# Holding back a transposing load, and moving one weight load and the first sigmoid, at the start of a gated feed-forward kernel

## The chip, the core and the metric

The kernel runs on one NeuronCore of one Trainium2 chip. The metric is the device time of one execution in microseconds (us); lower is better. TensorE does the matrix products, VectorE (DVE) and ScalarE (ACT) the work on their results, GpSimd (POOL) a little set-up; SyncE (SP) and ScalarE issue the transfers (DMAs) between the chip's main memory and the on-chip memory, each from a queue of its own. All transfers run on the same 16 DMA engines.

## The reference

```python
# x (32, 32, 512), w1 and w3 (512, 1792), w2 (1792, 512), all bf16
gate = einsum("bsd,df->bsf", x, w1)
up   = einsum("bsd,df->bsf", x, w3)
out  = einsum("bsf,fd->bsd", silu(gate) * up, w2)
```

There are 1024 tokens of width 512, and a hidden width of 1792. silu(g) is g times sigmoid(g).

## The kernel before

All of the hidden state is kept turned: the 128 partitions carry 128 of the 512 or 1792 features, and the free dimension carries tokens. So x is needed as `xT` (four slabs `dt` of 128 input features by 1024 tokens). It arrives in two ways. The first 256 tokens are loaded as they lie (`x_sb`, two loads of 128 tokens, L68 and L69), turned on TensorE by products with the identity (`turned`, L106) and copied to `xT` by VectorE and ScalarE (`put`, L116, in the order of `plan`, L140: slab 0 of tokens 0 to 127 by VectorE, slab 0 of tokens 128 to 255 by ScalarE, slab 1 by VectorE, slabs 2 and 3 by ScalarE). The other tokens are turned by the transfer itself: tokens 256 to 511 by the transposing load at L74, tokens 512 to 1023 by that at L78. The text calls them the first and the second transposing load.

The weights are whole in on-chip memory. Of w1 and w3 the first four column blocks of 128 (`FK` = 4) come ahead of the others: w1 in four loads of one slab each (L71, 128 KB; slabs 0 and 2 on SP's queue, 1 and 3 on ScalarE's), w3 in two loads of two slabs each (L72 and L73, 256 KB, both on SP's queue). They are called the first w3 half and the second w3 half. Behind the first transposing load, SP issues the remaining columns of w1 and w3 (L76 and L77), the second transposing load and w2 (L80, L81).

The instructions of each engine keep the order in which they are written (`manual_schedule`, L47); the framework adds the semaphore waits. TensorE's order is: six products of constants (`keep_warm`, L139), the eight turning products, then for the first 256 tokens all sixteen gate products slab by slab over four column blocks (L145 to L147), the sixteen up products likewise (L149 to L151), then the same column blocks for tokens 256 to 511 (L152 to L154), then the blocks 4 to 13 of the first 512 tokens, all 14 blocks of the other 512 (L157 to L163), and the output products with w2 (L165 to L177). So the order of need on TensorE is: x, w1 slabs 0 to 3, w3 slabs 0 to 3, the first transposing load, the other columns of w1 and w3, and much later the rest.

ScalarE's order is: three transfers (one x half, w1 slabs 1 and 3), a sigmoid of one element a partition that only serves to load the table of the function (L85), its two copies of the turned x, and then the 28 sigmoids and seven of the output copies. A sigmoid, a product of gate and sigmoid (L135) and a product with up (L136) follow each column block.

Of the kernel before, what the change touches and what calls it, by code (L numbers as in the profile page):

```python
# [10 lines left out]
def kernel(  # L11
# [8 lines left out]
    nc = tc.nc  # L20
    P = nc.NUM_PARTITIONS
    fp32 = mybir.dt.float32
    bf16 = mybir.dt.bfloat16
    SIGMOID = mybir.ActivationFunctionType.Sigmoid
# [3 lines left out]
    N = B * S  # L28
    NB = 512
    HB = NB // 2  # L30
    DT = D // P
    FT = F // P
# [4 lines left out]
    x_flat = x.flatten_outer_dims()  # L37
    out_flat = out.flatten_outer_dims()
    w1_v = w1.rearrange("(dt p) f -> p dt f", p=P)
    w3_v = w3.rearrange("(dt p) f -> p dt f", p=P)  # L40
    w2_v = w2.rearrange("(ft p) d -> p ft d", p=P)

    consts = ctx.enter_context(tc.tile_pool(name="consts", bufs=1))
# [9 lines left out]
    xT = consts.tile([P, DT, N], bf16, name="xT")  # L53
    w1_sb = consts.tile([P, DT, F], bf16, name="w1_sb")
    w3_sb = consts.tile([P, DT, F], bf16, name="w3_sb")
    w2_sb = consts.tile([P, FT, D], bf16, name="w2_sb")
    hT = consts.tile([P, FT, N], bf16, name="hT")

    FK = 4

    def load_x(queue, t0, t1):
        queue.dma_start(out=x_sb[:, t0:t1, :], in_=x_view[:, t0:t1, :])  # L62

    def load_w(queue, w_sb, w_v, c0, c1, d0=0, d1=DT):
        f0, f1 = c0 * P, c1 * P
        queue.dma_start(out=w_sb[:, d0:d1, f0:f1], in_=w_v[:, d0:d1, f0:f1])  # L66

    load_x(nc.sync, 0, 1)  # L68
    load_x(nc.scalar, 1, 2)  # L69
    for dt in range(DT):  # L70
        load_w(nc.sync if dt % 2 == 0 else nc.scalar, w1_sb, w1_v, 0, FK, dt, dt + 1)  # L71
    load_w(nc.sync, w3_sb, w3_v, 0, FK, 0, 2)  # L72
    load_w(nc.sync, w3_sb, w3_v, 0, FK, 2, DT)  # L73
    nc.sync.dma_start_transpose(out=xT[:, :, HB:NB], in_=x_flat[HB:NB, :])  # L74
    for c0, c1 in ((FK, 8), (8, FT)):
        load_w(nc.sync, w1_sb, w1_v, c0, c1)  # L76
        load_w(nc.sync, w3_sb, w3_v, c0, c1)  # L77
    nc.sync.dma_start_transpose(out=xT[:, :, NB:N], in_=x_flat[NB:N, :])  # L78
    FH = FT // 2
    nc.sync.dma_start(out=w2_sb[:, 0:FH, :], in_=w2_v[:, 0:FH, :])  # L80
    nc.sync.dma_start(out=w2_sb[:, FH:FT, :], in_=w2_v[:, FH:FT, :])  # L81

    one = nc.const_aps.tensor(1.0, [P, 1], bf16)
    table = consts.tile([P, 1], fp32, name="table")
    nc.scalar.activation(table[:], one, SIGMOID)  # L85

    def bank(name, tag="any"):
        return psum.tile([P, NB], fp32, name=name, tag=tag)
# [26 lines left out]
    def put(copy, pT, dts, nts):  # L115
        copy(  # L116
            xT[:, dts[0] : dts[-1] + 1, nts[0] * P : (nts[-1] + 1) * P],
            pT[:].rearrange("p d t c -> p d (t c)"),
        )
# [21 lines left out]
    parts = [turned(dts, nts) for _, dts, nts in plan]  # L141
    for pT, (copy, dts, nts) in zip(parts, plan):
        put(copy, pT, dts, nts)
    gates = [bank("gate_ps", "gate") for _ in range(FK)]
    for dt in range(DT):  # L145
        for fo in range(FK):
# [18 lines left out]
    for nt in range(NT):  # L165
        last = nt == NT - 1
        c0 = 0
        for DB in (D // 2, D // 4, D // 4) if last else (D,):
# [12 lines left out]
            else:  # L181
                nc.scalar.copy(o_sb[:], o_ps[:])  # L182
            nc.sync.dma_start(
                out=out_flat[nt * P : (nt + 1) * P, c0 : c0 + DB],
                in_=o_sb[:],
# [32 lines left out]
```

## Time and profile before

| what | us |
|---|---|
| median of 6 runs (lowest to highest) | 82.57 (81.89 to 82.89) |
| the profiled execution | 82.67 |
| its span, from the first to the last instruction | 80.9 |
| TensorE busy | 76.7 |
| VectorE busy | 39.5 |
| ScalarE busy | 23.1 |
| GpSimd busy | 0.7 |

The span is the part of the profiled execution that the trace sees; the other 1.77 us lie before its first and after its last instruction. In the views of the profile, PE is TensorE's matrix products and PEld its weight loads; ACTq and SPq are the queues' issuing of transfers by ScalarE and SyncE, in which the named duration is that of the issue and not of the transfer. A landing is the arrival of a transfer's sixteenth semaphore increment, one from each DMA engine. The profile tells for each issue how long after its start the landing came.

### The profile page before, as it was taken

The page shows a single profiled execution, that of the slowest core. Times are in us where ns is not written, and L with a number is a line of the kernel's source. Part 1 is how long each engine was busy: PE and PEld are TensorE (multiplying, and loading weights), DVE is VectorE, ACT ScalarE, POOL GpSimd, SP SyncE. Part 2 cuts the span into 40 slices and gives each one's busy share as a digit, 9 for nine tenths or more (in the row PEclk, how much of TensorE's full clock was granted, in tenths as well). Part 3 has the DMA queues.
Part 4 walks back from the last instruction along what each step waited for, and adds up shares of the span by engine and source line. Part 5 has one row for each costly group of instructions (what it writes and reads, how often), then busy time and mean ns, then how long its engine had stood idle before and what let it go on. Part 6 is the DMA issues. An engine that isn't in the chain of part 4 may idle for free.

```text
span 80.9 us, 1071 instructions
## 1 busy us (share of the span) xinstructions
PE 76.7 (95%) x410; PEld 39.1 (48%) x410; DVE 39.5 (49%) x61; ACT 23.1 (29%) x39; POOL 0.7 (1%) x6
## 2 busy tenths in 40 slices
PE   6979999999999999999999999999999999999960
PEld 2358884444444444444444444444444444444950
DVE  0120099989888878878868878872000000000130
ACT  0730265223442223442223432220220220220200
POOL 3000000000000000000000000000000000000000
DMA  0999999999990000000000000000101101101120
GB/s 19 279 308 224 321 360 376 291 111 326 349 286 0 0 0 0 0 0 0 8 4 0 0 0 0 0 4 0 44 21 65 52 21 65 48 17 65 53 61 16
DMA packets 9925, 7.67 MB, mean 95 GB/s; under 512 B 3776, under 2 KB 9920, under 8 KB 9920
## 3 DMA queue, kind: packets, MB, share of 16 engines
q1 hardware_dynamic: 9488, 7.21, 32.8%
q10 hardware_dynamic: 432, 0.39, 1.5%
q8 instruction: 3, 0.05, 0.2%
q14 instruction: 2, 0.02, 0.1%
HBM read 5.77 MB, written 1.05 MB: 84 GB/s over the span
## 4 chain that ended last, share of the span: by engine, by line
PE 89%; DMA 5%; SPq 1%; DVE 0%; issue 0%; DVEq 0%
PE o_ps L171 30%; PE up_ps L123 30%; PE gate_ps L123 29%; DMA w_sb<-in_w_dram 5%; SPq L66 1%; SPq L62 0%; DVE o_sb L180 0%; DVEq L180 0%
## 5 line engine op out<-in xcount | busy, mean ns | idle before, releaser
L123 PEld LDWEIGHTS <-w_sb 128*128 128x128 bf16 x256 | 25.0, 98 | 24.0 <-DMA w_sb<-in_w_dram 0.8
L123 PE MATMUL gate_ps<-xT,w_sb 128*128 128x512 bf16 (+1 forms) x128 | 29.3, 354 | 0.6 <-DMA w_sb<-in_w_dram 0.6
L123 PE MATMUL up_ps<-xT,w_sb 128*128 128x512 bf16 (+1 forms) x128 | 28.9, 352 | 0.0
L133 ACT ACTIVATE sig<-gate_ps 128x512 f32<-128x512 f32 x28 | 16.7, 597 | 31.7 <-PE gate_ps L123 30.6
L171 PE MATMUL o_ps<-w_sb,hT 128*128 128x512 bf16 (+2 forms) x140 | 24.4, 336 | 0.0
L135 DVE TENSOR_TENSOR t<-gate_ps,sig 128x512 f32<-128x512 f32 x28 | 19.3, 689 | 9.4 <-ACT sig L133 9.4
L136 DVE TENSOR_TENSOR hT<-t,up_ps 128x512 bf16<-128x512 f32 x28 | 19.3, 688 | 3.3 <-PE gate_ps L123 0.5
L171 PEld LDWEIGHTS <-hT 128*128 128x128 bf16 x140 | 12.6, 98 | 11.9
L180 DVE CAST o_sb<-o_ps 128x128 bf16<-128x128 f32 (+1 forms) x3 | 1.0, 336 | 22.3 <-PE o_ps L171 22.3
L182 ACT CAST o_sb<-o_ps 128x512 bf16<-128x512 f32 x7 | 4.1, 585 | 18.0 <-PE o_ps L171 18.0
L94 PE MATMUL warm_ps<-const-bfloat16-1.0 128*128 128x512 bf16 x6 | 2.7, 623 | 0.8 <-PEq L202 0.8
L116 DVE CAST xT<-pT 128x128 bf16<-128x128 f32 (+1 forms) x2 | 0.7, 358 | 3.9 <-PE pT L106 3.8
L85 ACT ACT_TABLE_LOAD x1 | 1.3, 1283 | 2.1 <-issue 2.1
L94 PEld LDWEIGHTS <-const-bfloat16-1.0 128*128 128x128 bf16 x6 | 0.7, 133 | 1.9 <-issue 1.9
L106 PEld LDWEIGHTS <-x_sb 128*128 128x128 bf16 x8 | 0.8, 136 | 0.9 <-DMA x_sb<-in_x_dram 0.9
L106 PE MATMUL pT<-ident,x_sb 128*128 128x128 bf16 x8 | 1.1, 308 | 0.0
L116 ACT CAST xT<-pT 128x128 bf16<-128x128 f32 (+1 forms) x2 | 0.8, 425 | 0.7 <-PE pT L106 0.7
masks.py:199 POOL TENSOR_SCALAR_AFFINE_SELECT ident<-ident 128x128 bf16<-128x128 bf16 x1 | 0.3, 293 | 0.1
masks.py:197 POOL MEMSET ident<- 128x128 bf16 x1 | 0.2, 204 | 0.3 <-POOLq L202 0.3
L85 ACT ACTIVATE table<-const-bfloat16-1.0 128x1 f32<-128x1 bf16 x1 | 0.2, 203 | 0.0
L202 POOL MEMSET const-bfloat16-1.0<- 128x1 bf16 x1 | 0.1, 101 | 0.0
L202 POOL MEMSET const-uint8-127<- 128x1 uint8 x1 | 0.1, 101 | 0.0
(2 smaller groups left out, 0.2 us busy)
## 6 DMA issues: line engine op xcount, KB each, us to landing
w_sb<-in_w_dram SPq DMA_DIRECT2D x2, 896.0 KB, 7.0
w_sb<-in_w_dram SPq DMA_DIRECT2D x2, 768.0 KB, 8.2
w_sb<-in_w_dram SPq DMA_DIRECT2D x2, 512.0 KB, 5.8
out_dram<-o_sb SPq DMA_DIRECT2D x7, 128.0 KB, 1.7
w_sb<-in_w_dram SPq DMA_DIRECT2D x2, 256.0 KB, 4.8
w_sb<-in_w_dram ACTq DMA_DIRECT2D x2, 128.0 KB, 4.0
w_sb<-in_w_dram SPq DMA_DIRECT2D x2, 128.0 KB, 3.7
x_sb<-in_x_dram ACTq DMA_DIRECT2D x1, 128.0 KB, 2.9
```

The lines of the kernel that those rows point to most:

```text
L66: queue.dma_start(out=w_sb[:, d0:d1, f0:f1], in_=w_v[:, d0:d1, f0:f1])
L85: nc.scalar.activation(table[:], one, SIGMOID)
L94: nc.tensor.matmul(warm_ps[:, 0:cols], lhsT=one.to_broadcast([P, P]), rhs=one.to_broadcast([P, cols]), start=True, stop=True,)
L106: nc.tensor.matmul(pT[:, i, j, :], lhsT=x_sb[:, nt, dt * P : (dt + 1) * P], rhs=ident[:], start=True, stop=True,)
L116: copy(xT[:, dts[0] : dts[-1] + 1, nts[0] * P : (nts[-1] + 1) * P], pT[:].rearrange("p d t c -> p d (t c)"),)
L123: nc.tensor.matmul(ps[:, c0 : c0 + n1 - n0], lhsT=w_sb[:, dt, fo * P : (fo + 1) * P], rhs=xT[:, dt, n0:n1], start=(dt == 0), stop=(dt == D ...
L133: nc.scalar.activation(sig[:], gate_ps[:], SIGMOID)
L135: nc.vector.tensor_mul(t[:], gate_ps[:], sig[:])
L136: nc.vector.tensor_mul(hT[:, fo, nb * NB : (nb + 1) * NB], t[:], up_ps[:])
L171: nc.tensor.matmul(o_ps[:], lhsT=hT[:, fo, nt * P : (nt + 1) * P], rhs=w2_sb[:, fo, c0 : c0 + DB], start=(fo == 0), stop=(fo == FT - 1),)
L180: nc.vector.tensor_copy(o_sb[:], o_ps[:])
L182: nc.scalar.copy(o_sb[:], o_ps[:])
```

## The change

The first transposing load and all that SP issues after it are written after the copies of the turned x. In front of it stands a copy of one element a partition on GpSimd, from column 0 of slab 0 of `xT` (which VectorE's first copy writes) to column 256 of slab 0, which the transposing load overwrites. So this copy waits for VectorE's first copy, and the transposing load waits for this copy. The second w3 half goes from SP's queue to ScalarE's, behind its three transfers. The sigmoid of one element, and with it the load of the function's table, stands ahead of ScalarE's transfers.

```diff
+    one = nc.const_aps.tensor(1.0, [P, 1], bf16)
+    table = consts.tile([P, 1], fp32, name="table")
+    nc.scalar.activation(table[:], one, SIGMOID)
+
     load_x(nc.sync, 0, 1)
     load_x(nc.scalar, 1, 2)
     for dt in range(DT):
         load_w(nc.sync if dt % 2 == 0 else nc.scalar, w1_sb, w1_v, 0, FK, dt, dt + 1)
     load_w(nc.sync, w3_sb, w3_v, 0, FK, 0, 2)
-    load_w(nc.sync, w3_sb, w3_v, 0, FK, 2, DT)
-    nc.sync.dma_start_transpose(out=xT[:, :, HB:NB], in_=x_flat[HB:NB, :])
-    for c0, c1 in ((FK, 8), (8, FT)):
-        load_w(nc.sync, w1_sb, w1_v, c0, c1)
-        load_w(nc.sync, w3_sb, w3_v, c0, c1)
-    nc.sync.dma_start_transpose(out=xT[:, :, NB:N], in_=x_flat[NB:N, :])
-    FH = FT // 2
-    nc.sync.dma_start(out=w2_sb[:, 0:FH, :], in_=w2_v[:, 0:FH, :])
-    nc.sync.dma_start(out=w2_sb[:, FH:FT, :], in_=w2_v[:, FH:FT, :])
-
-    one = nc.const_aps.tensor(1.0, [P, 1], bf16)
-    table = consts.tile([P, 1], fp32, name="table")
-    nc.scalar.activation(table[:], one, SIGMOID)
+    load_w(nc.scalar, w3_sb, w3_v, 0, FK, 2, DT)
...
     for pT, (copy, dts, nts) in zip(parts, plan):
         put(copy, pT, dts, nts)
+
+    nc.gpsimd.tensor_copy(xT[:, 0, HB : HB + 1], xT[:, 0, 0:1])
+    nc.sync.dma_start_transpose(out=xT[:, :, HB:NB], in_=x_flat[HB:NB, :])
+    for c0, c1 in ((FK, 8), (8, FT)):
+        load_w(nc.sync, w1_sb, w1_v, c0, c1)
+        load_w(nc.sync, w3_sb, w3_v, c0, c1)
+    nc.sync.dma_start_transpose(out=xT[:, :, NB:N], in_=x_flat[NB:N, :])
+    FH = FT // 2
+    nc.sync.dma_start(out=w2_sb[:, 0:FH, :], in_=w2_v[:, 0:FH, :])
+    nc.sync.dma_start(out=w2_sb[:, FH:FT, :], in_=w2_v[:, FH:FT, :])
+
     gates = [bank("gate_ps", "gate") for _ in range(FK)]
```

No product, sigmoid or output copy changes, and TensorE's and VectorE's instructions keep their order. The rest of SP's order (w1 and w3 columns, second transposing load, w2, outputs) stays as it is.

## The prediction

> **What bounds the kernel now.** I read the chain of waits first. From 6.09 us on it is TensorE without a break (gate, up and output products) to the last output copy; ahead of that stands one transfer.
>
> ```profile
> 1.60 0.05 issue
> 1.65 4.39 DMA w_sb<-in_w_dram
> 6.04 0.05 issue
> 6.09 1.05 PE gate_ps L123 x8
> 7.13 1.75 PE up_ps L123 x16
> 8.88 0.43 PE gate_ps L123 x4
> ```
>
> The columns are start, length and what. The transfer issued at 1.65 is w1 slab 2; it lands at 6.04. From here on any time won or lost before TensorE's unbroken run moves the end by as much. TensorE's timeline shows the stretch in question:
>
> ```profile
> 3.46 1.10 PE L106 MATMUL pT<-ident,x_sb 128*128 128x128 bf16 x8
> 4.35 1.18 PE L123 MATMUL gate_ps<-xT,w_sb 128*128 128x256 bf16 x8
> 6.09 1.05 PE L123 MATMUL gate_ps<-xT,w_sb 128*128 128x256 bf16 x8 [0.55 <-DMA w_sb<-in_w_dram]
> 6.97 1.91 PE L123 MATMUL up_ps<-xT,w_sb 128*128 128x256 bf16 x16
> 8.72 0.60 PE L123 MATMUL gate_ps<-xT,w_sb 128*128 128x256 bf16 x4
> ```
>
> The gates of slabs 0 and 1 start at 4.35, those of slabs 2 and 3 at 6.09 after a wait of 0.55 (shown as idle; the last product of the first group starts at 5.26 and the next could start 0.11 later, at 5.37, so 0.72 can be won). Up follows at 6.97 and the second 256 tokens at 8.72, with no idle time shown.
>
> Then the landings, each as start of issue plus time to landing, read line by line: w1 slab 3 1.66 + 4.56 = 6.22; first w3 half 2.12 + 4.66 = 6.78, needed 6.97; second w3 half 2.59 + 4.89 = 7.48, needed 7.84 (half of up's sixteen products after 6.97); first transposing load 3.60 + 4.95 = 8.55, needed 8.72. The margins are 0.19, 0.36 and 0.17 us: if gates ran 0.7 earlier, these three would be late next.
>
> ```profile
> L74 SPq DMA_TRANSPOSE xT<-in_x_dram x1: 1299/1299/1299, 3.6 to 3.6; - x1
> DMA to landing us min/median/max: 4.9/4.9/4.9
> ```
>
> Last, the table by stretches (PE, PEld, DVE, ACT, POOL busy; granted clock; DMA share; GB/s):
>
> ```profile
> 2.00:3.60 1.60, 1.60 (x5) 0.40 (x3) 0.00 (x0) 1.45 (x2) 0.00 (x0) 1.00 0.86 281
> 3.60:4.90 1.30, 1.30 (x12) 1.19 (x12) 0.72 (x2) 0.60 (x3) 0.00 (x0) 1.00 0.96 263
> 4.90:6.10 1.20, 0.65 (x7) 0.34 (x6) 0.00 (x0) 0.28 (x1) 0.00 (x0) 1.00 1.04 343
> ```
>
> The middle line is the window in which SP issues the first transposing load (1.30 us from 3.60). The engines were as busy as after it but moved 263 GB/s and not 343. The packet records agree: of the plain 1 KB packets that start between 2.2 and 8.0 us, all but one of those longer than 150 ns (the usual one takes 46) start between 3.68 and 4.97, one of them 1,172 ns long. The sixteen increments of w1 slab 2 come from 4.37 to 6.04: most DMA engines had it by 4.7, a few a microsecond later. So the issue of the transposing load seems to hold up what is in flight, on some engines badly.
>
> **The change, part by part.**
>
> *The hold.* VectorE's first copy ends at 3.78 + 0.29 = 4.07. GpSimd's copy of 128x1 is not in the trace; its rows bound it by 0.10 (setting 128x1) and 0.29 (the select on 128x128); I take 0.20, between them because it also reads. Hand-overs between engines cost about 0.07 (GpSimd's set ends 0.94, the select that waits for it starts 1.01). 4.07 + 0.07 + 0.20 + 0.07 = 4.41: the first transposing load is issued 0.81 later (0.7 to 0.9). Its window of 1.30 becomes 4.41 to 5.71. w1 slabs 2 and 3 are then mostly across (first increments 4.37 and 4.71), so their wait at 6.09 should nearly vanish: up to 0.72 won. But the two w3 halves, 512 KB, are now what is in flight during the issue: before, it was w1.
>
> Queued behind it on SP are the four loads of the other columns, the second transposing load and w2, all 0.8 later. Before, columns 4 to 7 of w1 and w3 landed at 4.95 + 5.43 = 10.38 and 5.58 + 6.26 = 11.84 for TensorE at 12.21 and 13.07, so 1.8 and 1.2 us cover the 0.8; without that cover the cost would be up to 0.8. The second transposing load (8.04 + 11.3 = 19.3, needed near 29.6) and w2 (24.5, needed 53.8) are far off. GpSimd has nothing behind the copy.
>
> *Second w3 half on ScalarE.* Its issue moves from 2.59 to about 2.2, which alone wins nothing: the engines were never short of issued work then. What changes is order. On one queue the first half was served ahead of the second, 6.78 and 7.48; on two queues the halves share the engines. The need has not changed: the first half is wanted 0.87 us before the second. Bounds for the first half's landing: at the late end 7.48, as the last of the pair today; at the early end 6.2, from 1.25 MB (1.31 million bytes: x, w1 and both halves) at 343 GB/s, 3.82 us, from 2.0, plus some 0.35 from an engine's last packet to its increment in the packet records. I take 7.25: the hold-up of the issue is moved onto these transfers, not removed, so the pair ends as today, and SP's half ends some 0.2 ahead, because ScalarE's queue starts a little later.
>
> The Trainium skill, DMA: Bandwidth & Descriptors, "Issuing engines are not separate DMA queues", speaks against this part: transfers from several engines interleave on the same 16 DMA engines, and a second issuer saves only issue time. This trace shows SP's and ScalarE's halves of w1 landing 0.18 apart (6.04 and 6.22), which is such sharing; by the rule alone the first half would land with the second, at 7.48 and not 7.25.
>
> *The sigmoid first.* Its table load (1.28) and the element (0.20) today run at 2.14 to 3.64, hidden before ScalarE's first copy at 3.96; moved, they are hidden again. The price is on the transfers behind them. Bounds: nothing, or 1.48 if the queue waits for both. The row for a queue running on past its engine:
>
> ```profile
> 2.14 1.28 ACT L85 ACT_TABLE_LOAD   x1 [2.14 <-issue]
> 3.44 0.20 ACT L85 ACTIVATE table<-const-bfloat16-1.0 128x1 f32<-128x1 bf16 x1
> ```
>
> The element starts 0.02 after the table load's end, so it stood ready: the queue had gone on. I take 0.10 for passing on two instructions. ScalarE's x half then lands at 3.69, and the first gate starts at 4.45; the gates of slab 1 end at 5.47, still before up can start.
>
> The skill's Perfetto Trace Analysis, "DVE / Act Engine Instruction", says that the sequencer is free once an instruction is in the wait queue; no row of this trace has a transfer issued behind a compute instruction on ScalarE.
>
> *The sum.* The gates of all four slabs end at 5.47 + 0.87 = 6.34. Up starts at 7.25 + 0.05 = 7.30, not 6.97: +0.33. The second w3 half (7.48, needed 8.17) and the first transposing load are then no bound: its packets today wait for the slowest engine to be done with w3, and it lands 8.55 again, needed 9.05. On the profiled execution 82.67 + 0.33 = 83.00; it lies 0.10 above the median of the runs, so for the median 82.57 + 0.33 = 82.90.
>
> **The rivals.**
> - *The gain comes through* (faster). If the moved issue holds up the w3 halves by its mean and not by its worst engine, 1.30 x (1 - 263/343) = 0.30, the pair is at 6.2 + 0.30 = 6.5 and up starts at 6.55: 82.57 - 0.42 = 82.15; with no hold-up, from 6.34: 81.95. It decides as soon as the first half lands before 6.92. For it: the lowest run, 81.89, is what the kernel needs with no such wait. Against: five of six runs cluster at 82.4 to 82.9, so the bad engine is the rule.
> - *ScalarE's queue waits for the table.* Its x half is 1.48 late; ScalarE's last copy of turned x ends 5.18 + 1.48 = 6.66, gates of slabs 2 and 3 start 6.7, up 7.58: +0.61, 83.2. Against: the two rows above.
> - *The hold is too long.* If the transposing load takes 4.95 from its issue wherever it starts, it lands at 4.41 + 4.95 = 9.36, and the second 256 tokens wait from 8.72 to 9.41: +0.69, 83.26. Against: its first packets start at 5.68, just when the w3 halves have passed on the quickest engine, so it waited in line.
> - *The hold does nothing* (the long packets have another cause): w1 slab 2 is as late as now, the w3 halves within their margins: 82.5 to 82.7.
>
> **How the numbers follow.** Forecast (wait moves from w1 to w3) 0.45, between +0.1 and +0.6, 82.7 to 83.2 on the median; gain comes through 0.30; table 0.10; hold too long 0.10; nothing 0.05. About 0.5%, 0.41 us, is what a measurement can tell from no change. Slower by more (above 82.98): 0.20 of the forecast's 0.45 and both dear rivals, 0.40. Faster by more (below 82.16): 0.25 of 0.30. Within: 0.25 + 0.05 + 0.05 = 0.35. The range holds 82.0 to 83.35: from just above the full gain to just above the rivals at 83.2 to 83.3.
>
> **What would show it.** Right: no idle time before the gates of slabs 2 and 3, w1 slab 2 landed before 5.3, an idle time before the first up product near 1 us, up's start near 7.3, and the first w3 half landing within 0.3 of the second. Long plain packets at 4.4 to 5.8. Wrong: up's start before 6.9 (the gain came through), ScalarE's first transfer issued after 1.5 (table), or idle time before the second 256 tokens (hold).

## The result and the profile after

| | before | after |
|---|---|---|
| median, us (lowest to highest, runs) | 82.72 (81.89 to 83.68, 36) | 83.49 (82.86 to 83.98, 17) |
| profiled execution, us | 82.67 | 83.98 |
| its span, us | 80.9 | 82.2 |
| start of the first up product in it, us | 6.97 | 8.31 |

The changed kernel is slower: the ratio is 1.0101, with a 95% interval from 1.0078 to 1.0124, some 0.84 us (0.77 between the two medians). The ratios, here and below, leave out executions that were disturbed, such as one of 411.71 us in d3_act_late. The 83.49 lies above the range of the prediction. The profiled execution of the changed kernel happens to be the longest of its 17 runs, so its numbers overstate what the typical run loses.

The chain of waits of the changed kernel up to the eighth microsecond, in order of time (start, length, what):

```profile
1.66 0.42 SPq L66
2.08 0.04 issue
2.12 6.14 DMA w_sb<-in_w_dram
8.26 0.05 issue
8.31 1.70 PE up_ps L115 x14
```

Before, the transfer on this chain was w1 slab 2. Now it is the one issued at 2.12, the first w3 half, which lands at 8.26, and the work that it releases is up and no longer the gates. TensorE's timeline shows both waits (start, length, instructions, and in brackets the idle time before them):

```profile
3.29 1.07 PE L98 MATMUL pT<-ident,x_sb 128*128 128x128 bf16 x8
...
6.94 1.05 PE L115 MATMUL gate_ps<-xT,w_sb 128*128 128x256 bf16 x8 [1.39 <-DMA w_sb<-in_w_dram]
8.31 1.92 PE L115 MATMUL up_ps<-xT,w_sb 128*128 128x256 bf16 x16 [0.33 <-DMA w_sb<-in_w_dram]
```

The gates of slabs 2 and 3 still wait, longer than before (1.39 for 0.55), and up waits as well. The shown idle time is short because the ends of products overlap; without a wait up starts 0.88 after these gates (6.09 and 6.97 before), so here it could have started at 7.82 and lost 0.49. After this TensorE has no gap that the earlier kernel didn't have, and it can be counted: profiled time less start of the first up product is 82.67 - 6.97 = 75.70 before and 83.98 - 8.31 = 75.67 after. In b1, b2, b5, f0, f1, g_after and g_act_26 below it is 75.65 to 75.71. So the start of up is the whole difference, 1.34 us in these two executions, and the median of 83.49 stands for a start of up near 83.49 - 75.67 = 7.82, hence a landing of the first w3 half near 7.77.

The page's list of transfers (queue, count, KB each, microseconds to landing) shows what became of the two halves, first after, then before:

```profile
w_sb<-in_w_dram SPq DMA_DIRECT2D x1, 256.0 KB, 6.1
w_sb<-in_w_dram ACTq DMA_DIRECT2D x1, 256.0 KB, 6.3
```

```profile
w_sb<-in_w_dram SPq DMA_DIRECT2D x2, 256.0 KB, 4.8
```

On one queue a half took 4.8 us from its issue; on two queues they took 6.1 and 6.3 and landed at 8.26 and 8.54, 0.28 apart and not 0.70.

What the change says of itself is there, in the order that was meant. GpSimd's, SP's and ScalarE's timelines:

```profile
3.99 0.19 POOL L137 COPY xT<-xT 128x1 bf16<-128x1 bf16 x1 [2.69 <-DVE xT L108]
```

```profile
4.21 1.30 SPq L138 DMA_TRANSPOSE xT<-in_x_dram  x1
```

```profile
0.73 1.28 ACT L70 ACT_TABLE_LOAD   x1 [0.73 <-PEq L205]
0.79 0.40 ACTq L62 DMA_DIRECT2D x_sb<-in_x_dram  x1
...
2.19 0.46 ACTq L66 DMA_DIRECT2D w_sb<-in_w_dram  x1
```

The copy that holds the first transposing load takes 0.19; the load is issued at 4.21 instead of 3.60; ScalarE's first transfer goes out 0.06 after the table load has begun, and the second w3 half at 2.19.

### The profile page after: what moved, and what is told of

Same layout as the page of the kernel before. It is cut to its first block, busy times and chain, and to the rows that moved or that the text cites. A ratio compares the mean times of both kernels' runs of the same rounds, so it can differ in the third digit from the quotient of the medians.

```text
span 82.2 us, 1073 instructions
## 1 busy us (share of the span) xinstructions
PE 76.9 (94%) x410; PEld 39.2 (48%) x410; DVE 39.4 (48%) x61; ACT 23.1 (28%) x39; POOL 0.9 (1%) x7
## 2 busy tenths in 40 slices
DMA packets 9925, 7.67 MB, mean 93 GB/s; under 512 B 3776, under 2 KB 9920, under 8 KB 9920
## 4 chain that ended last, share of the span: by engine, by line
PE 87%; DMA 7%; SPq 2%; issue 0%; DVE 0%; DVEq 0%
PE up_ps L115 30%; PE o_ps L174 30%; PE gate_ps L115 27%; DMA w_sb<-in_w_dram 7%; SPq L66 1%; SPq L62 0%; DVE o_sb L183 0%; DVEq L183 0%
```

## The experiments

There were seventeen runs: fourteen further kernels, and the kernel before, the changed one and f1's once more. One table has the readings; the sections below have the edits, what was expected, and what follows. The landings and the start of up are of one profiled execution of each kernel, the ratio to the kernel before is of all its runs.

| kernel | w1 slab 2 | first w3 half | second w3 half | first half less slab 2 | up starts | ratio (95%) |
|---|---|---|---|---|---|---|
| before | 6.04 | 6.78 | 7.48 | 0.74 | 6.97 | |
| f0_before | 6.24 | 6.97 | 7.67 | 0.73 | 7.17 | (one execution) |
| b1_hold | 5.78 | 6.61 | 7.32 | 0.83 | 7.23 | 1.0001 (0.9972 to 1.0031) |
| b3_sig | 5.17 | 6.84 | 7.61 | 1.67 | 6.89 | 1.0014 (0.9985 to 1.0042) |
| b5_hold_sig | 6.43 | 7.15 | 7.82 | 0.72 | 7.36 | 0.9998 (0.9968 to 1.0029) |
| after | 6.89 | 8.26 | 8.54 | 1.37 | 8.31 | 1.0101 (1.0078 to 1.0124) |
| g_after | 5.68 | 7.07 | 7.34 | 1.39 | 7.11 | 1.0101 (1.0039 to 1.0164) |
| b2_w3act | 7.16 | 8.53 | 8.72 | 1.37 | 8.57 | 1.0123 (1.0088 to 1.0159) |
| c2_swap | 6.90 | 8.49 | 8.29 | 1.59 | 8.54 | 1.0116 (1.0048 to 1.0184) |
| f1_act_26 | 6.39 | 7.77 | 8.05 | 1.38 | 7.82 | 1.0059 (1.0025 to 1.0093) |
| g_act_26 | 5.35 | 7.05 | 7.28 | 1.70 | 7.10 | 1.0075 (1.0036 to 1.0113) |
| b4_w3act_sig | 6.04 | 6.85 | 9.34 | 0.81 | 7.28 | 1.0148 (1.0097 to 1.0199) |
| f2_dose | 6.21 | 6.92 | 7.82 (its last slab) | 0.71 | 7.14 | 1.0000 (0.9966 to 1.0034) |
| c1_late | 5.12 | 5.89 | 8.80 | 0.77 | 6.21 | 1.0242 (1.0150 to 1.0335) |
| d3_act_late | 5.78 | 6.47 | 8.22 | 0.69 | 6.71 | 1.0071 (1.0038 to 1.0104) |
| d1_w3b_copy | 5.69 | 6.35 | 8.16 | 0.66 | 6.62 | 1.0057 (1.0026 to 1.0089) |
| d2_w3b_x | 5.13 | 6.09 | 6.92 | 0.96 | 6.13 | 1.0019 (0.9986 to 1.0052) |
| c4_w3hold | 4.87 | 6.93 | 7.94 | 2.06 | 7.07 | 1.0102 (1.0053 to 1.0152) |
| c3_one | 5.28 | 6.93 | 7.87 | 1.65 | 6.98 | 1.0073 (1.0038 to 1.0108) |

The first column of landings scatters by as much as 1.2 us between two executions of one kernel (6.89 and 5.68 for the changed one). So no conclusion below rests on a single landing; those used are differences within an execution that come back in several, and the ratios.

### The parts one at a time

b1_hold: before, with the hold alone.

```diff
-    nc.sync.dma_start_transpose(out=xT[:, :, HB:NB], in_=x_flat[HB:NB, :])
...
         put(copy, pT, dts, nts)
+    nc.gpsimd.tensor_copy(xT[:, 0, HB : HB + 1], xT[:, 0, 0:1])
+    nc.sync.dma_start_transpose(out=xT[:, :, HB:NB], in_=x_flat[HB:NB, :])
```

(SP's later transfers move with it.)

> The kernel before with the hold alone (GpSimd copy of one column, first transposing load and all behind it after the copies of the turned x; second w3 half still on SP, sigmoid where it was). Theory Q (second queue): the whole loss comes from the second w3 half passing the w1 slabs and the first w3 half on DMA engines that lag, so the hold alone costs nothing: ratio to before 0.995 to 1.003, w1 slab 2 landed near 6.0, first w3 half near 6.8. Theory H (hold): the issue of the transposing load, moved to 4.2 to 5.5, now holds up the w3 halves, so the hold alone costs most of the loss: ratio 1.005 to 1.010, first w3 half landed at 7.4 or later.

b2_w3act: before, with the second w3 half alone on ScalarE's queue.

```diff
-    load_w(nc.sync, w3_sb, w3_v, 0, FK, 2, DT)
+    load_w(nc.scalar, w3_sb, w3_v, 0, FK, 2, DT)
```

> The kernel before with the second w3 half on ScalarE's queue alone (transposing load not held, sigmoid behind ScalarE's transfers). Theory Q: most of the loss is here: ratio 1.006 to 1.012, w1 slabs 2 and 3 landed 0.5 to 0.9 later than before (6.0 and 6.2), the two w3 halves within 0.4 of one another at 8.0 or later. Theory H: ratio 0.998 to 1.004, w1 slabs 2 and 3 landed as before.

b3_sig: before, with the first sigmoid ahead of ScalarE's transfers and nothing else.

```diff
+    one = nc.const_aps.tensor(1.0, [P, 1], bf16)
+    table = consts.tile([P, 1], fp32, name="table")
+    nc.scalar.activation(table[:], one, SIGMOID)
     load_x(nc.sync, 0, 1)
```

> The kernel before with the sigmoid of one element ahead of ScalarE's transfers alone. Theories Q and H: ScalarE's first transfer issued at about 0.79 and not 0.73, no difference in time: ratio 0.997 to 1.003. A third theory A (the table load at the start of the span disturbs the transfers) expects a ratio over 1.004.

b4_w3act_sig: the edits of b2 and b3 together, that is, the changed kernel without its hold.

> The changed kernel without the hold: second w3 half on ScalarE's queue and the sigmoid first. Theory Q: as slow as the changed kernel, ratio 1.006 to 1.012. Theory H: ratio 0.998 to 1.004. If both parts are needed (the transposing load must meet a w3 half on the other queue), the hold was put there to help: the ratio is then above the changed kernel's 1.010.

b5_hold_sig: the changed kernel with the second w3 half back on SP's queue.

```diff
-    load_w(nc.scalar, w3_sb, w3_v, 0, FK, 2, DT)
+    load_w(nc.sync, w3_sb, w3_v, 0, FK, 2, DT)
```

> The changed kernel with the second w3 half back on SP's queue (hold and sigmoid first stay). All theories that put the loss on that move: ratio 0.997 to 1.003. If hold and sigmoid cost only together: over 1.004.

Measured: the hold alone 1.0001, the sigmoid alone 1.0014, both together 0.9998, the w3 half alone 1.0123. So the whole loss belongs to the one line that moves the second w3 half. TensorE's timeline of b2_w3act is that of the changed kernel over again:

```profile
7.20 1.05 PE L123 MATMUL gate_ps<-xT,w_sb 128*128 128x256 bf16 x8 [1.35 <-DMA w_sb<-in_w_dram]
8.57 1.05 PE L123 MATMUL up_ps<-xT,w_sb 128*128 128x256 bf16 x8 [0.33 <-DMA w_sb<-in_w_dram]
```

b1_hold also tests the reason on which the prediction's gain and its new wait were both built. SP's timeline, the stretch from 3.60 to 4.90 (PE, PEld, DVE, ACT, POOL busy; granted clock; DMA share; GB/s) and TensorE's timeline of it:

```profile
4.34 1.31 SPq L137 DMA_TRANSPOSE xT<-in_x_dram  x1
```

```profile
3.60:4.90 1.30, 1.30 (x11) 1.14 (x11) 0.72 (x2) 0.61 (x3) 0.19 (x1) 1.00 0.89 234
```

```profile
4.36 3.03 PE L114 MATMUL gate_ps<-xT,w_sb 128*128 128x256 bf16 x16
7.23 1.91 PE L114 MATMUL up_ps<-xT,w_sb 128*128 128x256 bf16 x16
```

The transposing load's issue is out of the first half of that stretch, and the engines still moved only 234 GB/s there. Of its plain 1 KB packets that start between 3 and 7 us, those longer than 150 ns start from 3.59 to 5.19, where before they started from 3.68 to 4.97. The same stretch of the changed kernel, whose transposing load is issued at 4.21, gives 208 GB/s in one execution and 320 in the other (after, then g_after):

```profile
3.60:4.90 1.30, 1.30 (x11) 1.11 (x10) 0.72 (x2) 0.77 (x2) 0.19 (x1) 1.00 0.84 208
```

```profile
3.60:4.90 1.30, 1.30 (x11) 1.11 (x12) 0.72 (x2) 0.68 (x2) 0.19 (x1) 1.00 1.06 320
```

So the slow stretch begins without the transposing load's issue, and how slow it is differs between executions of one kernel. Two other runs agree. In d3_act_late below the load is issued at 5.55, and the first long packets start from 3.70 to 4.53. In b4_w3act_sig it is issued at 2.60, and no packet that starts from 2.4 to 3.6 is long; the next long ones start from 3.64 on.

The start of up in b1, 7.23, is no sign of a late transfer: w1 slab 2 had landed at 5.78 and the first w3 half at 6.61. The row shows sixteen gate products in 3.03 us, where c1_late below needs 2.05. Until 6.5 TensorE's weight loads for them take 151 ns each and come 0.21 apart, afterwards 98 ns and 0.11. What the hold is worth is therefore read from the ratio and not from this row.

b4 can't be read as the changed kernel without its hold. Its ScalarE timeline has the second w3 half issued at 3.33, though ScalarE was free at 2.2:

```profile
3.33 0.39 ACTq L66 DMA_DIRECT2D w_sb<-in_w_dram  x1
```

At 3.31 SP's half of x lands. In this order of transfers the second w3 half got the completion semaphore of that load and had to wait for it. It then left behind the transposing load (issued at 2.60), landed at 9.34, and up's third slab waited for it. What the hold is worth beside a second half on ScalarE's queue therefore stays open; b2 (1.0123, no hold) and the changed kernel (1.0101) overlap.

### Order or queue

Is it ScalarE's queue that is slow, or the loss of the order? c2_swap: before, with the halves' queues exchanged the other way: the first w3 half on ScalarE's queue, the second on SP's.

```diff
-    load_w(nc.sync, w3_sb, w3_v, 0, FK, 0, 2)
+    load_w(nc.scalar, w3_sb, w3_v, 0, FK, 0, 2)
```

> The kernel before with the first w3 half on ScalarE's queue and the second on SP's (nothing else changed). Theory R: as slow as with the second half there, ratio 1.008 to 1.014, w1 slabs 2 and 3 landed at 6.7 or later. Theory P (priority: what costs is that the first half loses its place ahead of the second): w1 slabs 2 and 3 land as before, only the first up product is late, ratio 1.002 to 1.007.

c1_late: the changed kernel, with the second w3 half, still on ScalarE's queue, issued only after VectorE's first copy, behind a one-column copy on GpSimd into it.

```diff
-    load_w(nc.scalar, w3_sb, w3_v, 0, FK, 2, DT)
...
         put(copy, pT, dts, nts)
+    nc.gpsimd.tensor_copy(w3_sb[:, 2, 0:1], xT[:, 0, 0:1])
+    load_w(nc.scalar, w3_sb, w3_v, 0, FK, 2, DT)
     nc.gpsimd.tensor_copy(xT[:, 0, HB : HB + 1], xT[:, 0, 0:1])
```

> The changed kernel with the second w3 half still on ScalarE's queue, but issued only once VectorE's first copy is done (about 4.2 instead of 2.2; held by a one-column GpSimd copy like the transposing load). Theory R (two queues with a backlog at once, from 3.5 to 5, make some DMA engines lag): w1 slab 2 lands at 5.2 to 6.1 as before, ratio 0.997 to 1.005. Theory C (it is ScalarE's queue as such, or the order in which the halves land): as slow as the changed kernel, ratio over 1.007.

d1_w3b_copy: before, with the second w3 half on SP's queue, released by VectorE's first copy as in c1, and the transposing load behind it.

```diff
+    nc.gpsimd.tensor_copy(w3_sb[:, 2, 0:1], xT[:, 0, 0:1])
     load_w(nc.sync, w3_sb, w3_v, 0, FK, 2, DT)
     nc.sync.dma_start_transpose(out=xT[:, :, HB:NB], in_=x_flat[HB:NB, :])
```

(All three stand after the copies of the turned x.)

> The kernel before with the second w3 half held (instead of moved to the other queue): on SP's queue ahead of the first transposing load, released by VectorE's first copy, issued near 4.2. Theory B (a backlog of 512 KB of w3 behind w1 makes engines lag, and 256 KB doesn't): w1 slabs 2 and 3 land by 5.4, first w3 half by 6.2, up starts near 6.3, second half about 7.0 (needed 7.2): ratio 0.992 to 1.000. If the late issue costs more than the lag: the second half lands after 7.6, ratio 1.002 to 1.008.

d3_act_late: c1, with the transposing load held by ScalarE's last copy instead, so that it follows the second w3 half.

```diff
-    nc.gpsimd.tensor_copy(xT[:, 0, HB : HB + 1], xT[:, 0, 0:1])
+    nc.gpsimd.tensor_copy(xT[:, 1, HB : HB + 1], xT[:, 3, HB - 1 : HB])
```

> The changed kernel with the second w3 half on ScalarE's queue, held until VectorE's first copy as in c1_late, and the first transposing load held longer, until ScalarE's last copy of the turned x, so that it no longer passes that half. Theory B: w1 and the first half as in c1_late (5.1 to 5.4, 5.9), second half by 7.2, first transposing load by 8.6: ratio 0.994 to 1.003, so ScalarE's queue as such costs nothing. Theory C (ScalarE's queue as such): ratio over 1.007.

Measured: with the queues exchanged (c2) the ratio is 1.0116. I use that ratio alone, since its profiled execution is the slowest of its four. With the second half late, the order is kept and it is the same on either queue: d1 on SP's 1.0057, d3 on ScalarE's 1.0071, landings 8.16 and 8.22, and the same wait at up's third slab (TensorE's timelines, d1 and then d3):

```profile
8.30 1.03 PE L113 MATMUL up_ps<-xT,w_sb 128*128 128x256 bf16 x8 [0.64 <-DMA w_sb<-in_w_dram]
```

```profile
8.35 1.03 PE L113 MATMUL up_ps<-xT,w_sb 128*128 128x256 bf16 x8 [0.60 <-DMA w_sb<-in_w_dram]
```

So ScalarE's queue as such costs nothing that these runs can tell; running beside the first half costs. In d1, d3 and c1 the first half lands 0.66 to 0.77 after slab 2, as before, and up starts at 6.21 to 6.71. TensorE's timeline of c1:

```profile
4.32 2.05 PE L113 MATMUL gate_ps<-xT,w_sb 128*128 128x256 bf16 x16
6.21 1.04 PE L113 MATMUL up_ps<-xT,w_sb 128*128 128x256 bf16 x8
8.94 1.03 PE L113 MATMUL up_ps<-xT,w_sb 128*128 128x256 bf16 x8 [1.69 <-DMA w_sb<-in_w_dram]
```

Gates and the first half of up run without a wait, and then everything is given back, because the second half comes late: it was issued at 4.63, just behind the transposing load (4.32), and 49 of its 256 packets of 1 KB took 160 to 674 ns beside the transposing ones. The profiled execution, 83.72, is the quickest of c1's four; the others took 84.91 to 85.03, and no trace shows where they lost the rest of the 1.0242.

### Less in flight behind w1

If long transfers behind w1 make it late, fewer of them should help. d2_w3b_x: before, with the second w3 half on SP's queue held until SP's half of x has landed.

```diff
     load_w(nc.sync, w3_sb, w3_v, 0, FK, 0, 2)
+    nc.gpsimd.tensor_copy(w3_sb[:, 2, 0:1], x_sb[:, 0, 0:1])
     load_w(nc.sync, w3_sb, w3_v, 0, FK, 2, DT)
```

> As d1, but released earlier, by the landing of SP's half of x (issued near 3.6). Theory B: the best of both: w1 and the first w3 half land as in d1, the second half by 6.8: ratio 0.990 to 0.998. If the backlog counts from 3.6 on however it came about: w1 slab 2 near 6 again, ratio 0.998 to 1.004.

c4_w3hold: before, with both halves and all behind them held by VectorE's first copy.

```diff
+    nc.gpsimd.tensor_copy(w3_sb[:, 0:DT:2, 0], xT[:, 0, 0:2])
     load_w(nc.sync, w3_sb, w3_v, 0, FK, 0, 2)
     load_w(nc.sync, w3_sb, w3_v, 0, FK, 2, DT)
     nc.sync.dma_start_transpose(out=xT[:, :, HB:NB], in_=x_flat[HB:NB, :])
```

(All after the copies.)

> The kernel before with both w3 halves and all behind them held until VectorE's first copy is done (issued from about 4.2 on SP). If w3's transfers are what makes engines lag with w1: w1 slabs 2 and 3 land by 5.2, few plain packets longer than 150 ns between 3.5 and 5; up then waits for w3 until 7.0 or so: ratio 0.998 to 1.006. If the lag is w1's own: w1 slab 2 lands near 6 again and everything is 0.5 to 1.0 later, ratio 1.006 to 1.014.

c3_one: before, with all four w1 slabs on SP's queue.

```diff
-        load_w(nc.sync if dt % 2 == 0 else nc.scalar, w1_sb, w1_v, 0, FK, dt, dt + 1)
+        load_w(nc.sync, w1_sb, w1_v, 0, FK, dt, dt + 1)
```

> The kernel before with all four w1 slabs on SP's queue (ScalarE issues only its half of x). Theory R: with one backlog the lagging engines catch up: w1 slab 2 lands before 5.7 although it is issued 0.45 later, the slabs land in order, ratio 0.990 to 1.000. If issue time is what bounds (SP then issues one transfer each 0.45 us): w3 halves 0.5 to 0.9 later than before, ratio 1.003 to 1.010.

Measured: with nothing (c4) or one half (c1, d2) behind it, slab 2 lands at 4.87, 5.12 and 5.13, and the slow stretch carries 344 and 345 GB/s in c1 and d2. But d1 and d3, also with one half, have 5.69 and 5.78, and b3, with both, has 5.17. That points to the amount in flight without settling it. Nor does it pay: in c4 up waits 1.09 for the first half, and d2, whose TensorE timeline is the best of all up to 12 us, gives it back at the next columns:

```profile
4.21 2.01 PE L124 MATMUL gate_ps<-xT,w_sb 128*128 128x256 bf16 x16
6.13 1.96 PE L124 MATMUL up_ps<-xT,w_sb 128*128 128x256 bf16 x16
...
11.47 1.03 PE L124 MATMUL gate_ps<-xT,w_sb 128*128 128x512 bf16 x3
12.83 1.04 PE L124 MATMUL up_ps<-xT,w_sb 128*128 128x512 bf16 x4 [0.33 <-DMA w_sb<-in_w_dram]
```

Up starts 0.84 earlier than before (6.13 for 6.97), the gates of the later blocks 0.74 earlier (11.47 for 12.21), but their up products wait for columns 4 to 7 of w3 and start at 12.83 for 13.07: 0.24 is left in this execution, and nothing in the median, 1.0019 (0.9986 to 1.0052). This is the nearest to a better kernel that was found; none beat the kernel before. In c3 up waits 0.52 for the first half, landed at 6.93: 1.0073, slower.

### The size of the term

f1_act_26: the changed kernel, with the second half on ScalarE's queue issued at 2.51 instead of 2.19, about where SP issued it before, behind four GpSimd settings of an unused tile and a one-column copy. g_act_26 is the same kernel again, beside g_after, the changed kernel again; f0_before is the kernel before, profiled again.

```diff
+    idle = consts.tile([P, P], bf16, name="idle")
+    for _ in range(4):
+        nc.gpsimd.memset(idle[:], 0.0)
+    nc.gpsimd.tensor_copy(w3_sb[:, 2, 0:1], idle[:, 0:1])
     load_w(nc.scalar, w3_sb, w3_v, 0, FK, 2, DT)
```

> The changed kernel with the second w3 half still on ScalarE's queue, held until about 2.6 (the time at which SP issued it before) by four GpSimd sets and a one-column copy. Theory 2Q (two queues with a backlog at once): as slow as the changed kernel, ratio 1.007 to 1.013, w1 slab 2 at 6.5 or later. Theory E (it was issued 0.4 earlier, and the backlog behind w1 grew earlier): as before, ratio 0.998 to 1.004, w1 slab 2 near 6.0.

> The kernel of f1_act_26 again (second w3 half on ScalarE's queue, issued near 2.5 instead of 2.2). Sharing alone: ratio 1.004 to 1.008, w1 slab 2 at 6.0 to 6.5 as in the kernels with that half on SP, first w3 half at 7.6 or later.

> The changed kernel again, beside g_act_26 on one chip. If sharing between the two w3 halves is the whole loss, it is as slow as g_act_26 (the two ratios within 0.002). If its second w3 half, issued 0.4 us earlier, also makes the lagging engines lag longer: ratio 1.009 to 1.013, at least 0.003 above g_act_26, and w1 slab 2 at 6.6 or later.

> The kernel before unchanged, a second look at its landings. If the first profile was typical: w1 slab 2 lands at 5.2 to 6.1, before any of the runs with the second w3 half free on ScalarE's queue (6.9 to 7.2).

f2_dose: the changed kernel, with only slab 3 of w3 (128 KB) on ScalarE's queue and slab 2 on SP's.

```diff
-    load_w(nc.scalar, w3_sb, w3_v, 0, FK, 2, DT)
+    load_w(nc.sync, w3_sb, w3_v, 0, FK, 2, 3)
+    load_w(nc.scalar, w3_sb, w3_v, 0, FK, 3, DT)
```

> The changed kernel with only the second half's slab 3 (128 KB) on ScalarE's queue, slab 2 on SP's behind the first half. Theory 2Q: about half of the loss, ratio 1.003 to 1.007. If any w3 transfer on ScalarE's queue is enough: ratio over 1.008. If nothing under 256 KB matters: 0.998 to 1.002.

Measured: f1 1.0059 and g_act_26 1.0075, with up waiting in both; g_after 1.0101, the same as the changed kernel's first result. TensorE's timelines of g_after and of f1, in this order:

```profile
4.25 2.53 PE L115 MATMUL gate_ps<-xT,w_sb 128*128 128x256 bf16 x16
7.11 1.92 PE L115 MATMUL up_ps<-xT,w_sb 128*128 128x256 bf16 x16 [0.34 <-DMA w_sb<-in_w_dram]
```

```profile
6.43 1.05 PE L118 MATMUL gate_ps<-xT,w_sb 128*128 128x256 bf16 x8 [1.27 <-DMA w_sb<-in_w_dram]
7.82 1.92 PE L118 MATMUL up_ps<-xT,w_sb 128*128 128x256 bf16 x16 [0.34 <-DMA w_sb<-in_w_dram]
```

The same wait of 0.33 to 0.34 ahead of up stands in after, b2, g_after and f1, whether slab 2 landed at 7.16 or at 5.68. In f0_before, as in the first profile of before, slab 2 is late (6.24) and up has no wait. f2 is no measure of a half dose: its slab 3 was issued only at 3.14, after SP's half of x had landed at 3.12, as in b4; so little ran beside the first half, and its 1.0000 agrees with the rest without adding to it.

## Why the prediction was off

**What held.** The direction, the largest of the three chances. That on two queues the halves share and land almost together: 0.28 apart after, 0.19 to 0.28 in the four profiles with the clean wait, against 0.67 to 0.77 with both issued on SP's queue in before, f0, b1, b3 and b5. The Trainium skill, DMA: Bandwidth & Descriptors, "Issuing engines are not separate DMA queues", which the prediction held against this part, has transfers from several engines interleave, and that row bears it out; the issue time that a second issuer saves was worth nothing here, since 0.40 us earlier made nothing arrive earlier. The hold: copy 0.19 for 0.20; transposing load issued at 4.21 for 4.41, because VectorE's first copy ended sooner. The load landed at 9.38, just where the rival in which the hold is too long had it (9.36), but for a need at 10.07; in g_after, where up starts at 7.11, it landed at 8.13 for a need at 8.87. So it takes no fixed time from its issue (5.17 and 3.92), and the rival falls. Columns 4 to 7 of w1 and w3 were issued 0.61 and 1.33 later (5.56 and 6.91), not 0.8, and came in time, since nothing after the start of up got longer. The rival of ScalarE's queue waiting for the table falls too: its first transfer was issued at 0.79 for 0.73 before, 0.06 later and not the 1.48 of the table load and the element. That agrees with what the Trainium skill, Perfetto Trace Analysis, "DVE / Act Engine Instruction", says of a sequencer that is free once an instruction stands in the wait queue, and it is now shown by a row.

**The step that failed: "their wait at 6.09 should nearly vanish".** It rested on "the issue of the transposing load seems to hold up what is in flight". The long packets and the low rate of 263 GB/s did fall into the 1.30 us of that issue, but by coincidence: in b1 the issue is moved to 4.34 and long packets still start from 3.59, slab 2 lands at 5.78, and the time is 1.0001; in d3 it is moved to 5.55, and they start from 3.70. (The reading of the packets was also off by one: of those that start between 2.2 and 8.0 two lie outside, at 2.74 and 7.99.) The gates' wait stayed, 1.39 after and 1.27 in f1; g_after shows none, with slab 2 landed at 5.68. Of the signs that the prediction named for being right, the halves' landing within 0.3 came and slab 2 before 5.3 didn't. What makes the packets from 3.5 on long stays open. It is not the transposing load's issue; the landing of slab 2 differs by 1.2 us between two executions of one kernel. Whether an issue adds long packets of its own isn't settled: in d3, between 4.53 and 5.74 none starts, and from 5.74 to 6.37, within the issue, eight do.

**The term that was mis-sized: the first half's landing, 7.25.** It was set by "the pair ends as today, and SP's half ends some 0.2 ahead", an absolute end taken from one execution. The measured pair ended at 8.54, and by the median the first half landed at about 7.77. (0.15 of the distance from 82.90 to 83.49 is the base: six runs of the kernel before had a median of 82.57, thirty-six have 82.72.) The quantity that repeats is the distance from w1 slab 2. With both halves on SP's queue it is 0.72 to 0.83 in before, f0, b1 and b5 (1.67 in b3, where slab 2 was early); with the second on ScalarE's queue beside it, 1.37, 1.39, 1.37 and 1.38 in after, g_after, b2 and f1 (1.70 in g_act_26). The growth of some 0.64 is near what sharing would make of it, as an estimate: a half is 256 packets of 1 KB, 16 on each of 16 engines, at 46 ns each 0.74 us, and between slab 2 and the end of the first half there now lie the packets of two halves and not of one. The gates of slabs 2 and 3 cover 0.88 of it (the hand-over of 0.05 stands on both sides). Before, 0.74 is under that and up doesn't wait; after, 1.37 is over it, and 1.37 - 0.88 = 0.49 is the wait that the timeline shows. Reckoned from the trace of before alone, slab 2 at 6.04 plus its 0.74 to the first half plus 0.74 for the other half's packets gives a landing of 7.52 and up at 7.57: 82.57 + 0.60 = 83.17, clearly slower, where the prediction had 82.90.

**What remains.** 0.49 of the 0.84 is shown; f1 and g_act_26, at 0.59% and 0.75% (0.49 and 0.62 us, with intervals that reach from 0.2 to 0.9), are about that. The other 0.2 to 0.35 would have to be a later slab 2, as far as the traces go. Its landing was 6.89 and 7.16 in two profiles with the half issued early, but 5.68 in the third. By the medians, taking 75.67 and 75.70 off, up starts at 7.82 after and 7.02 before, so slab 2 would have landed near 7.82 - 1.42 = 6.40 and 7.02 - 0.93 = 6.09, if it set the start in both. Whether the earlier issue, at 2.19, takes its share from w1 too isn't settled: 1.0101 (1.0039 to 1.0164) stands beside 1.0075 (1.0036 to 1.0113).

The prediction also took TensorE's pace from its one trace, and let all gates end by 6.34. In b1 and b4 its first products were so slow that up started at 7.23 and 7.28 although w1 and the first w3 half had landed by 6.61 and 6.85. How often that happens in executions without a trace isn't known.

**The range.** Its upper end, 83.35, stood just above the rivals at 83.2 to 83.3, and none of them let the first half land later than 7.48, the end of the pair in the one trace. That would be up at 7.53 and 83.13; for a pair that ends later as a whole there was no room.

## What to carry to other kernels

Transfers that are needed one after the other belong on one queue in that order; put on two, the first one here shared the engines with the second and arrived with it, and what counts is whether the work ahead of its need still covers that (0.88 covered 0.74, not 1.37). Measure landings relative to the transfer ahead, over several executions, before an absolute one is put into a sum; a slow stretch that happens to coincide with an issue is no proof of its cause until the issue has been moved. Ask of every earlier start what else it takes bandwidth from, and look one wait further: in the runs here what was won at the gates was given back at up, at its second half or at the next columns.

## What the runs showed of the hardware

- A transposing load seems to go when its slowest engine does: in the changed kernel 19 of its 256 B packets took 600 to 1,800 ns, from 6.35 on, until about 8.15, where 18 ns is usual. In the kernel before, such packets took 400 to 1,180 ns until 7.30, and the second w3 half just ahead of it on the queue got its sixteen increments within 7.40 to 7.48.
- Plain packets that run beside transposing ones can be slow: 49 of the second w3 half's 256 in c1, all started from 6.2 to 7.5, took 160 to 674 ns, for the usual 46.
- A transfer can wait for an unrelated earlier one, without any instruction that says so: in b4 and f2 the load on ScalarE's queue was issued 0.02 us after SP's half of x had landed (3.33 after 3.31, 3.14 after 3.12), since both shared a completion semaphore. In the kernel before, the first transposing load itself went so: SP was free at 3.06 and issued it at 3.60, 0.02 after ScalarE's half of x had landed at 3.59.
- TensorE's first products run at about half their later pace, and for how long differs between executions of one kernel: in g_act_26 the weight loads took some 147 ns each until 4.4, in f1, the same kernel, 98 ns from 3.6 on, and in b1 151 ns until 6.5. The granted clock in b1's row reads 1.00 all the same.
